# The order of all 3,359 operations of a clustered-attention and Mish-FFN kernel, taken from a written list

## The chip, the cores and the metric

The kernel runs on one core of a Trainium2 chip. The metric is the device time of one execution in microseconds, from the unprofiled runs; the profile is of one further execution.

## The reference, cut to what matters

Queries, keys and values have 4 batches, 8 heads, 768 positions and 64 features. Every query and key is assigned to one of 16 clusters of its head by the largest product of its normalised vector with the normalised centroids. A query attends to the keys of its own cluster. The result, 3072 tokens by 512, goes through a feed-forward block with a Mish-like gate of width 2048.

```python
    mask = q_assign[:, :, :, None] == k_assign[:, :, None, :]
    scores = scale * np.matmul(q, k.transpose(0, 1, 3, 2))
    scores = np.where(mask, scores, -1000000000.0)
    scores = scores - np.max(scores, axis=-1, keepdims=True)
    attn = np.exp(scores)
    attn = attn / (np.sum(attn, axis=-1, keepdims=True) + 1e-09)
    return np.matmul(attn, v).astype(np.float32)
...
    h = x @ w_in
    sp = np.where(h > 20.0, h, np.log1p(np.exp(np.minimum(h, 20.0))))
    g = h * np.tanh(sp)
    return (g @ w_out).astype(np.float32)
```

## The kernel before, in words

**Work.** A unit is one head of one batch and one of three blocks of 256 queries: 96 units, numbered 0 to 95, each with two halves of 128 queries. A product of two float32 matrices is made of float16 (or float32r) high and low parts, three matmuls for one. The operations of a half, `(i, a)`, in the order in which they need each other, with their first lines:

- `scores` (L625, PE): four matmuls into a two-bank PSUM tile, of which there are two. Its operands come from `prep_hi` (L477), `prep_lo` (L491) and copies by DMA or ACT (`copy_t`, `copy_z`, `copy_a`, `copy_b`, `hot_copy`); the cluster mask is an extra 16 rows made by the `assign_*` operations (L536 on).
- `rowmax` (L645, DVE), `expo` (L651, ACT, the Exp, with the row sum), `total` and `recip` (POOL or DVE, DVE).
- `p_hi` (L692, POOL) and `p_lo` (L704, DVE): high and low halves of the probabilities, and `ptrans` (L719), which transposes them by a DMA from the SP queue. For the first 24 units (pairs 0 to 11) `p_lo` transposes on PE instead, and `ptrans` copies from PSUM.
- `pv` (L737, PE): the product with the values, for a pair of units `m` (2m, 2m+1), in three parts of twelve matmuls; one PSUM tile.
- `pv_out` (L778, ACT) and `x_lo` (L806, DVE): the two halves of the feed-forward block's input.

The feed-forward block works on tiles of 256 tokens. `m1` (L818, PE) is half a tile of the hidden layer, twelve matmuls, two halves to a PSUM tile, of which there are two; `e_mish` (L836, ACT) applies Mish and frees the tile; `e_gh` (L847, POOL) and `e_gl` (L854, DVE) split it; `m2` (L957, PE) is one of eight parts of six matmuls that add up to an output tile; `m_out` and `m_store` write it. Hidden tiles `j` come in pairs: the even `e_mish` loads the Mish table first (L842), the odd one loads the Exp table behind it (L845). The last tiles, 72 to 95, use a Strassen-like scheme: sums of weight blocks (`c_whole`, `c_sums`, `c_high`, `c_low`, L1007 to L1037), sums of activations (`n_*`, `l_*`), and products `n_mul` (L906) and `k_mul` (L1106), whose results are combined and stored.

In the first 170 us the weights are also prepared: `w_load`, `w_abs`, `w_low`, `w_f32`, `w_sq` (a Gram matmul for the norm), `w_hi`, `w_lo`, and the centroids are normalised: `put_consts` (L154) makes constants, `centroids` (L178) and `cent_put` (L203) the operand for the assignment.

**Order.** Each operation is a small function, entered in a plan with a time key: a formula with constants of the tables `T` (L1371) and `N` (L1504), plus an entry of `SHIFT` (L1561), a dictionary with single corrections. The plan sorts by key and issues; a function that needs another's result calls `pl.after`, which issues that one first if it is still open. After every operation, `tie` pins each new instruction behind the last one of its engine (and DMA queue), so each of the five engines works in exactly the order of issue; what one engine waits for on another is left to semaphores.

```python
    def at(self, t, fn, *args):
        op = fn.__name__, *args
        self.ops[op] = (t + SHIFT.get(op, 0), len(self.ops), fn, args)
...
    def run(self):
        for op in sorted(self.ops, key=lambda op: self.ops[op][:2]):
            self.issue(op)
```

`ring` (L1001) is called by three functions of the tail that take a tile from the pool of three `pt` tiles; it issues the last user of the tile three before, if that is still open:

```python
    def ring(*last):

        while len(rings) >= 3 and pl.state.get(rings[-3]) != "done":
            pl.after(rings[-3])
        rings.append(last)
```

Of the kernel before, what the change touches and what calls it, by code (L numbers as in the profile page):

```python
# [25 lines left out]

class Plan:
# [27 lines left out]
    def tie(self):  # L55
# [17 lines left out]
def tile_clustered_attention_mish_ffn(  # L73
# [9 lines left out]
    nc = tc.nc  # L83
    pool = lambda name, bufs, **kw: ctx.enter_context(tc.tile_pool(name=name, bufs=bufs, **kw))
# [22 lines left out]
    pl = Plan(tc)  # L107
# [891 lines left out]
    rings = []  # L999

    def ring(*last):  # L1001

        while len(rings) >= 3 and pl.state.get(rings[-3]) != "done":
            pl.after(rings[-3])
        rings.append(last)

    def c_whole(f):  # L1007
        pl.after(("pv", NU // 2 - 1, 2), ("w_lo", 8 + f))
        ring("c_low", f)
# [96 lines left out]
    def k_mul(t, n, f):  # L1106
# [3 lines left out]
        if f == 0:  # L1110
# [3 lines left out]
            else:  # L1114
                banks(("k", t))
                ring("k_12", t)
# [1194 lines left out]
```

## Time and profile before

| | us |
|---|---|
| unprofiled runs: median of 3 (lowest to highest) | 856.79 (856.72 to 857.35) |
| span of the profiled execution | 858.6 |
| PE busy (matmuls) | 837.1 |
| DVE busy | 702.6 |
| ACT busy | 520.9 |
| POOL busy | 428.0 |

The profiled execution's own time is its span, first to last instruction; it stands 1.8 us above the median of the unprofiled runs. PE is TensorE's matmuls, DVE VectorE, ACT ScalarE, POOL GpSimd, SP the queue that issues most DMAs. An engine's idle time is shown with what ended it. The profile's busy time of PE counts a matmul to its modelled end, so two matmuls that overlap count once and a stall shorter than the tail of a matmul does not show.

### The profile page before, as it was taken

The page shows a single profiled execution, that of the slowest core. Times are in us where ns is not written, and L with a number is a line of the kernel's source. Part 1 is how long each engine was busy: PE and PEld are TensorE (multiplying, and loading weights), DVE is VectorE, ACT ScalarE, POOL GpSimd, SP SyncE. Part 2 cuts the span into 40 slices and gives each one's busy share as a digit, 9 for nine tenths or more (in the row PEclk, how much of TensorE's full clock was granted, in tenths as well). Part 3 has the DMA queues.
Part 4 walks back from the last instruction along what each step waited for, and adds up shares of the span by engine and source line. Part 5 has one row for each costly group of instructions (what it writes and reads, how often), then busy time and mean ns, then how long its engine had stood idle before and what let it go on. Part 6 is the DMA issues. An engine that isn't in the chain of part 4 may idle for free.

```text
span 858.6 us, 17602 instructions
## 1 busy us (share of the span) xinstructions
PE 837.1 (97%) x6742; PEld 621.0 (72%) x6743; DVE 702.6 (82%) x1225; ACT 520.9 (61%) x885; POOL 428.0 (50%) x410
## 2 busy tenths in 40 slices
PE   8999899999999999999999999999999999999998
PEld 3776676776777777776776776776777776788887
DVE  7989989898889798788877798788978777699851
ACT  6878887765665666564565665465565564356520
POOL 1464665786567546556566447566566444110000
PEclk9999999999999999999999999999999999999999
DMA  9855672398889987897789977988887876000010
GB/s 348 262 173 165 193 209 54 73 180 170 149 153 194 193 154 133 156 184 141 145 177 181 172 157 120 171 155 165 130 159 136 139 137 128 24 1 2 1 44 32
DMA packets 253060, 121.51 MB, mean 142 GB/s; under 512 B 230288, under 2 KB 230800, under 8 KB 252976
## 3 DMA queue, kind: packets, MB, share of 16 engines
q1 hardware_dynamic: 247632, 108.46, 61.1%
q10 hardware_dynamic: 5344, 11.93, 6.3%
q8 instruction: 53, 0.87, 0.4%
q14 instruction: 31, 0.25, 0.1%
HBM read 35.72 MB, written 6.29 MB: 49 GB/s over the span
## 4 chain that ended last, share of the span: by engine, by line
PE 70%; DVE 13%; issue 5%; ACT 4%; DMA 4%; POOL 3%; ACTq 0%; POOLq 0%; DVEq 0%; SPq 0%
PE h L832 8%; PE h L833 8%; PE h L834 8%; PE o L753 8%; PE O L969 6%; PE O L971 6%; PE O L970 6%; PE s L631 5%; PE s L636 5%; DVE m L648 4%; PE cn L922 2%; DVE hl L717 2%; DMA pt<-hl 2%; ACT p L662 2%; PE as L543 1%
## 5 line engine op out<-in xcount | busy, mean ns | idle before, releaser
L662 ACT ACTIVATE p<-s,m 128x768 f32<-128x768 f32 x192 | 172.6, 899 | 161.4 <-DVE m L648 108.0
L700 POOL TENSOR_SCALAR hl<-p,l 128x768 f16<-128x768 f32 x144 | 167.1, 1163 | 168.0 <-DVE l L682 74.2
L648 DVE TENSOR_REDUCE m<-s 128x1 f32<-128x768 f32 x192 | 181.4, 949 | 30.2 <-PE s L636 28.1
L717 DVE SCALAR_TENSOR_TENSOR hl<-p,l,hl 128x768 f16<-128x768 f32 x144 | 172.4, 1202 | 12.2 <-POOL hl L700 11.7
L832 PE MATMUL h<-x,w 128*128 128x256 f16 x640 | 175.6, 274 | 1.5 <-ACT u L843 0.8
L833 PE MATMUL h<-x,w 128*128 128x256 f16 x640 | 174.4, 273 | 0.0
L834 PE MATMUL h<-x,w 128*128 128x256 f16 x640 | 174.4, 273 | 0.0
L631 PE MATMUL s<-A,B 128*128 128x384 f32 x384 | 117.3, 386 | 1.8 <-DMA B<-T 0.8
L969 PE MATMUL O<-w,g 128*128 128x512 f16 x288 | 109.6, 380 | 0.0
L971 PE MATMUL O<-w,g 128*128 128x512 f16 x288 | 109.2, 379 | 0.0
L970 PE MATMUL O<-w,g 128*128 128x512 f16 x288 | 109.2, 379 | 0.0
L636 PE MATMUL s<-Z,T 80*128 80x384 f32 x384 | 99.2, 339 | 0.4 <-issue 0.4
L832 PEld LDWEIGHTS <-w 128*128 128x128 f16 x768 | 75.1, 98 | 26.9 <-issue 17.3
L849 POOL TENSOR_SCALAR g<-u,mscg 128x512 f16<-128x512 f32 x72 | 70.3, 980 | 38.4 <-ACT u L843 36.0
L857 DVE SCALAR_TENSOR_TENSOR g<-u,mscg,g 128x512 f16<-128x512 f32 x72 | 75.5, 1050 | 12.2 <-POOL g L849 11.9
L833 PEld LDWEIGHTS <-w 128*128 128x128 f16 x768 | 75.5, 98 | 11.1 <-issue 1.6
L753 PE MATMUL o<-pt,v 128*64 128x256 f16 x1296 | 79.3, 274 | 3.6 <-DMA pt<-hl 3.0
L834 PEld LDWEIGHTS <-w 128*128 128x128 f16 x768 | 75.2, 98 | 8.6
L753 PEld LDWEIGHTS <-v 128*64 128x64 f16 x1296 | 68.4, 110 | 14.1 <-issue 9.6
L631 PEld LDWEIGHTS s<-A,B 128*128 128x128 f32 x384 | 61.9, 190 | 15.8 <-issue 4.9
L636 PEld LDWEIGHTS s<-Z,T 80*128 80x128 f32 x384 | 69.7, 189 | 0.9 <-DMA Z<-stg 0.7
L843 ACT ACTIVATE u<-h,msch 128x512 f32<-128x512 f32 x80 | 52.1, 685 | 25.0 <-PE h L834 14.5
(242 smaller groups left out, 1366.3 us busy)
## 6 DMA issues: line engine op xcount, KB each, us to landing
qk<-in_qk_dram SPq DMA_DIRECT2D x32, 384.0 KB, 4.6
stage<-in_w_in_dram SPq DMA_DIRECT2D x16, 512.0 KB, 6.6
stage<-in_w_out_dram SPq DMA_DIRECT2D x16, 512.0 KB, 4.5
vraw<-in_vP_dram SPq DMA_DIRECT2D x16, 384.0 KB, 5.2
T<-A ACTq DMA_DIRECT2D x30, 192.0 KB, 3.0
Z<-B SPq DMA_DIRECT2D x30, 192.0 KB, 3.4
B<-T ACTq DMA_DIRECT2D x28, 192.0 KB, 3.4
out_dram<-osb SPq DMA_DIRECT2D x18, 256.0 KB, 2.7
```

The lines of the kernel that those rows point to most:

```text
L631: nc.tensor.matmul(s[:, j, :384], st["B", n][:, q0 : q0 + P], st["A", n][:, j * 384 : (j + 1) * 384], start=True, stop=False,)
L636: nc.tensor.matmul(s[:, j, :384], st["T", n][: D + NCL, q0 : q0 + P], st["Z", n][: D + NCL, j * 384 : (j + 1) * 384], start=False, stop=True,)
L648: nc.vector.tensor_reduce(m, st["s", i, a][:, :, :384], axis=AX.XY, op=ALU.max, negate=True)
L662: nc.scalar.activation(p.rearrange("p (n x) -> p n x", n=2), st["s", i, a][:, :, :384], AF.Exp, bias=st["m", i, a], scale=1.0, accum_out=l,)
L700: nc.gpsimd.tensor_scalar(t[:, 0], p, r, 1.0, op0=ALU.mult, op1=ALU.mult)
L717: nc.vector.scalar_tensor_tensor(t[:, 1], p, r, t[:, 0], op0=ALU.mult, op1=ALU.subtract)
L753: nc.tensor.matmul(o[s * D : s * D + D, :256], v if early else v[:, int(part == 1)], st["pt", 2 * m + s][:, :, c + (0 if early or part < 2 ...
L832: nc.tensor.matmul(o, wh, xh, start=(c == 0), stop=False)
L833: nc.tensor.matmul(o, wh, xl, start=False, stop=False)
L834: nc.tensor.matmul(o, wl, xh, start=False, stop=(c == 3))
L969: nc.tensor.matmul(o, gh, wh, start=(f == 0 and fi == 0), stop=False)
L970: nc.tensor.matmul(o, gh, wl, start=False, stop=False)
```

## The change

The time keys and `SHIFT` (728 lines) are replaced by one list, `ORDER`, with all 3,359 operations; an operation's key is its place in the list. `ring` and its three calls go. Pools are wrapped in a class `Ring`, which notes each request for a tile, so that `tie` can pin the first instruction behind a request after the first instruction behind the one before from the same pool and tag, also where the two are on different engines. Work, shapes, engines and tiles of every operation stay. The formulas for the keys stay in the text but are no longer used.

```diff
+class Ring:
...
+    def tile(self, *args, tag=None, **kw):
+        if tag is None:
+            return self.pool.tile(*args, **kw)
+        self.asked.append((len(self.traced), (id(self), tag)))
+        return self.pool.tile(*args, tag=tag, **kw)
...
-        self.ops[op] = (t + SHIFT.get(op, 0), len(self.ops), fn, args)
+        self.ops[op] = (RANK[op], len(self.ops), fn, args)
...
-        for ins in self.traced[self.seen :]:
+        for n, ins in enumerate(self.traced[self.seen :], self.seen):
+            while self.asked and self.asked[0][0] <= n:
+                _, key = self.asked.pop(0)
+                if self.taken.get(key, ins.name) != ins.name:
+                    self.tc.add_manual_dep(ins, self.taken[key], order, reason="tile order")
+                self.taken[key] = ins.name
...
-        ring("c_low", f)
...
-        ring("l_sl", f)
...
-                ring("k_12", t)
...
-SHIFT = {
-    ('expo', 11, 0): -0.001, ('w_load', 10): -0.351, ('pv_out', 18): -0.443, ('scores', 24, 1): -0.221,
...
+ORDER = """
+qk_load 1, qk_load 0, qk_load 3, qk_load 2, centroids, put_consts, cent_put, prep_hi 1, prep_lo 1, prep_hi 0, v_load 0
+1, v_load 0 3, w_load 1, w_load 3, w_load 0, v_load 0 2, assign_mm 0, prep_lo 0, copy_z 1, copy_z 0, assign_turn 0,
+assign_max 0, assign_hot 0, assign_back 0, assign_put 0, copy_t 0, copy_a 0, copy_t 1, v_sq 0 3, copy_a 1, hot_direct
+1, copy_b 0, w_abs 1, v_sq 0 1, hot_direct 0, w_abs 3, v_sq 0 2, w_abs 0, w_load 2, v_load 0 0, w_load 7, w_load 4,
...
+w_f32 10, w_f32 13, w_f32 9, recip 5 1, w_f32 17, rowmax 7 1, w_abs 14, ptrans 6 0, rowmax 7 0, qk_load 6, copy_z 3,
...
+0, x_lo 21, p_hi 23 0, p_lo 23 0, scores 24 0, v_scale 1, rowmax 24 0, recip 23 1, ptrans 23 0, copy_t 9, moe_scale_h
+0, expo 24 0, m1 0 0, total 20 0, recip 20 0, prep_lo 9, p_hi 23 1, v_high 0 0, v_split 0 0, p_lo 23 1, v_split 0 1,
+rowmax 24 1, total 24 0, recip 24 0, ptrans 23 1, w_hi 14, expo 24 1, w_lo 14, pv 11 0, pv 11 1, total 21 0, recip 21
...
+recip 26 0, total 26 1, e_gl 0, rowmax 27 0, e_gl 1, recip 26 1, m2 0 0 0, scores 28 0, m1 3 1, m2 0 0 1, scores 27 1,
+total 23 0, recip 23 0, expo 27 0, copy_t 10, e_mish 2, e_mish 3, p_hi 26 0, prep_lo 10, p_hi 26 1, total 27 0, rowmax
+28 0, p_lo 26 0, v_split 1 0, recip 27 0, rowmax 27 1, ptrans 24 1, qk_load 13, ptrans 25 1, ptrans 25 0, copy_z 10,
+p_hi 27 0, v_high 1 1, e_gh 2, e_gh 3, pv 12 0, pv 12 1, pv 12 2, m1 4 0, m1 5 0, m1 4 1, expo 28 0, copy_b 10, pv_out
...
+recip 19 0, e_mish 4, expo 28 1, copy_a 10, expo 29 0, total 28 1, p_lo 28 0, recip 28 1, total 29 0, rowmax 29 1,
+recip 29 0, m1 7 0, scores 30 1, m1 5 1, scores 31 0, pv 13 0, pv 13 1, pv 13 2, m1 7 1, scores 30 0, m1 6 0, m1 6 1,
+scores 31 1, expo 29 1, e_mish 5, e_gh 4, p_hi 28 1, prep_hi 11, p_hi 29 0, p_lo 28 1, total 29 1, rowmax 30 1, rowmax
...
+RANK = {}
+for _n, _op in enumerate(" ".join(ORDER.split()).split(", ")):
+    _name, *_args = _op.split()
+    RANK[_name, *map(int, _args)] = _n
```

## Rows read from the trace of the kernel before

**Rows 1.** The page, first part: span, then each engine's busy time.

```profile
span 858.6 us, 17602 instructions
...
PE 837.1 (97%) x6742; PEld 621.0 (72%) x6743; DVE 702.6 (82%) x1225; ACT 520.9 (61%) x885; POOL 428.0 (50%) x410
```

**Rows 2.** Stretches: length, busy time by engine, granted clock, DMA share, GB/s.

```profile
0.00:27.80 27.80, 23.46 (x129) 12.79 (x130) 22.80 (x52) 20.32 (x38) 5.76 (x15) 1.00 0.93 336
27.80:157.80 130.00, 122.39 (x964) 89.55 (x963) 119.34 (x222) 105.04 (x209) 74.37 (x90) 1.00 0.55 161
157.80:177.60 19.80, 18.59 (x148) 14.67 (x147) 18.70 (x28) 13.75 (x23) 14.70 (x14) 1.00 0.68 114
...
200.00:740.00 540.00, 536.21 (x4288) 386.36 (x4287) 437.28 (x729) 317.25 (x517) 310.01 (x272) 1.00 0.83 153
740.00:820.00 80.00, 80.00 (x718) 69.99 (x716) 74.23 (x146) 45.23 (x71) 4.35 (x6) 1.00 0.01 5
```

**Rows 3.** Waits of PE, 200 to 740 us: total, times, longest.

```profile
PE o L753 <- DMA pt<-hl: 2.6, 3, 1.3
PE s L631 <- DMA B<-T: 0.8, 1, 0.8
```

**Rows 4.** Waits of DVE, 20 to 160 us: total, times, longest.

```profile
DVE m L648 <- PE s L636: 3.3, 4, 1.0
DVE l L680 <- POOL l L674: 1.9, 2, 1.0
```

**Rows 5.** Timeline of DVE, 0 to 24 us: start, duration, operation, idle before.

```profile
4.47 0.22 DVE L181 TENSOR_TENSOR csq<-csb 128x64 f32<-128x64 f32 x1 [0.83 <-DMA csb<-in_cent_dram]
...
9.92 0.98 DVE L554 STREAM_TRANSPOSE D<-as 128x768 f32<-128x768 f32 x1 [0.18 <-PE as L543]
```

**Rows 6.** Timeline of ACT, 4 to 20 us.

```profile
5.51 0.92 ACT L481 ACTIVATE A<-qk,scq 128x768 fp32r<-128x768 f32 x1
...
7.65 0.26 ACT L207 COPY C<-ct 64x128 f32<-64x128 f32 x1 [0.36 <-PE ct L201]
```

**Rows 7.** Timeline of DVE, 45 to 54 us.

```profile
48.26 0.17 DVE L680 RECIPROCAL l<-l 128x2 f32<-128x2 f32 x1 [0.90 <-POOL l L674]
...
51.51 0.96 DVE L648 TENSOR_REDUCE m<-s 128x1 f32<-128x768 f32 x1 [0.89 <-PE s L636]
```

**Rows 8.** Timeline of PE, 496 to 503 us: a pv, then two m2.

```profile
497.85 2.15 PE L753 MATMUL o<-pt,v 128*64 128x256 f16 x36
499.94 0.39 PE L969 MATMUL O<-w,g 128*128 128x512 f16 x1
...
502.54 0.27 PE L832 MATMUL h<-xx,w 128*128 128x256 f16 x1
```

**Rows 9.** Timeline, 454 to 463.5 us: an m1 half, a scores, the next m1.

```profile
455.54 0.28 PE L832 MATMUL h<-x,w 128*128 128x256 f16 x1
...
456.78 0.59 PE L631 MATMUL s<-A,B 128*128 128x384 f32 x2
...
457.57 0.28 PE L832 MATMUL h<-x,w 128*128 128x256 f16 x1
```

**Rows 10.** The page, fifth part: groups, count | busy, mean ns | idle before.

```profile
L662 ACT ACTIVATE p<-s,m 128x768 f32<-128x768 f32 x192 | 172.6, 899 | 161.4 <-DVE m L648 108.0
L700 POOL TENSOR_SCALAR hl<-p,l 128x768 f16<-128x768 f32 x144 | 167.1, 1163 | 168.0 <-DVE l L682 74.2
...
L849 POOL TENSOR_SCALAR g<-u,mscg 128x512 f16<-128x512 f32 x72 | 70.3, 980 | 38.4 <-ACT u L843 36.0
```

**Rows 11.** The chain that ended last, in order of time: start, duration, what.

```profile
456.86 5.70 DMA pt<-hl
```

**Rows 12.** Timeline of ACT, 476 to 483 us: an Exp, then a pair of e_mish.

```profile
479.29 0.19 ACT L662 ACTIVATION_READ_ACCUMULATOR p<-s,m 128x1 f32 x1
479.49 1.28 ACT L842 ACT_TABLE_LOAD   x1
480.79 1.26 ACT L843 ACTIVATE u<-h,msch 128x512 f32<-128x512 f32 x2
```

More of the change, by code (lines that the diff above doesn't have):

```diff
@@ new lines @@
+copy_t 7, w_abs 31, total 13 0, recip 13 0, rowmax 18 1, recip 16 1, rowmax 18 0, recip 17 1, w_f32 31, ptrans 17 1,
+w_sq 30, pv 8 0, w_sq 31, w_sum 1, expo 18 0, p_hi 18 0, p_lo 18 0, scores 19 0, w_spread 1, expo 18 1, ptrans 18 0,
+v_sq 1 0, v_sq 1 3, p_hi 18 1, w_scale 1, rowmax 19 0, p_lo 18 1, scores 19 1, pv 8 1, pv 8 2, total 18 1, w_hi 8,
+rowmax 19 1, ptrans 18 1, recip 18 1, expo 19 0, expo 19 1, pv_out 16, pv_out 17, w_lo 8, total 19 1, qk_load 8,
+v_load 1 2, copy_z 7, hot_copy 7, qk_load 9, qk_load 10, assign_mm 2, p_hi 19 0, assign_turn 2, prep_hi 8, prep_lo 8,
@@ new lines @@
+18 0, m1 18 1, scores 43 1, m1 20 0, m2 1 1 5, pv_out 38, pv_out 39, expo 42 0, expo 42 1, v_sq 2 1, copy_t 15, x_lo
+38, x_lo 39, total 42 0, p_lo 40 0, rowmax 43 0, total 42 1, p_lo 41 1, v_split 1 3, e_gl 16, recip 42 0, recip 42 1,
+scores 44 1, m2 1 1 6, assign_mm 4, p_hi 42 1, p_hi 42 0, p_lo 42 1, rowmax 43 1, ptrans 41 1, ptrans 40 0, ptrans 42
+1, v_load 2 0, hot_copy 15, expo 43 0, e_mish 18, copy_a 15, expo 43 1, e_gl 17, total 43 0, recip 43 0, p_lo 42 0,
+total 43 1, recip 43 1, assign_turn 4, rowmax 44 1, pv 20 0, p_hi 43 1, e_gh 18, p_hi 43 0, prep_hi 16, prep_lo 16, pv
@@ new lines @@
+52 0, m_out 2 1, expo 52 1, scores 53 0, m1 28 1, m2 3 0 0, scores 53 1, m1 29 0, m1 29 1, p_lo 51 1, e_gl 26, total
+52 0, p_lo 50 1, total 52 1, recip 52 1, e_gl 27, rowmax 53 1, recip 52 0, rowmax 53 0, ptrans 51 0, ptrans 50 0,
+copy_z 18, ptrans 51 1, hot_copy 18, ptrans 50 1, copy_b 18, expo 53 1, e_mish 28, e_mish 29, expo 53 0, m2 3 0 1, pv
+25 0, pv 25 1, pv 25 2, p_hi 52 1, p_hi 52 0, prep_hi 19, prep_lo 19, e_gh 29, pv_out 50, scores 54 0, m2 3 0 2,
+scores 54 1, m1 30 0, m1 31 0, m2 3 0 3, scores 55 0, m1 30 1, scores 55 1, m1 31 1, p_lo 52 0, p_lo 52 1, total 53 0,
@@ new lines @@
+32 0, pv 32 1, pv 32 2, m2 4 1 5, scores 68 1, m1 43 0, m1 43 1, m2 4 1 6, scores 68 0, m2 4 1 7, m1 45 0, m1 44 0, m1
+44 1, pv_out 64, pv_out 65, copy_b 23, e_mish 42, e_mish 43, p_hi 67 0, p_hi 67 1, e_gh 43, prep_hi 24, e_gh 42, e_gl
+40, p_lo 67 0, x_lo 65, v_split 2 3, assign_turn 6, assign_max 6, p_lo 67 1, x_lo 64, rowmax 68 1, assign_hot 6,
+rowmax 68 0, assign_back 6, expo 68 1, m_out 4 1, expo 68 0, copy_t 24, assign_put 6, scores 69 0, m2 5 0 0, total 68
+0, total 68 1, recip 68 1, recip 68 0, e_gl 42, assign_stg 6, prep_lo 24, p_hi 68 0, p_hi 68 1, scores 69 1, m1 45 1,
@@ new lines @@
+recip 79 0, p_hi 79 0, e_gh 54, e_gh 55, ptrans 76 0, qk_load 29, ptrans 77 0, copy_z 27, ptrans 77 1, hot_copy 27,
+ptrans 76 1, ptrans 78 0, m2 6 0 5, scores 80 0, pv 38 0, pv 38 1, pv 38 2, copy_b 27, p_lo 79 0, e_gl 54, rowmax 80
+0, total 79 1, p_lo 78 1, e_gl 55, recip 79 1, assign_mm 7, m2 6 0 6, scores 80 1, copy_a 27, expo 80 0, pv_out 76,
+pv_out 77, p_hi 79 1, prep_hi 28, prep_lo 28, x_lo 76, x_lo 77, total 80 0, assign_turn 7, p_lo 79 1, rowmax 80 1, m1
+59 0, scores 81 1, m2 6 0 7, scores 81 0, m1 56 0, m1 56 1, m2 6 1 0, scores 82 0, m2 6 1 1, m_store 5 1, ptrans 79 0,
@@ new lines @@
+copy_t 30, e_mish 62, e_mish 63, pv_out 84, pv_out 85, expo 87 1, expo 88 0, e_gh 63, prep_lo 30, p_hi 87 0, e_gh 62,
+x_lo 85, x_lo 84, e_gl 62, p_lo 87 0, total 87 1, total 88 0, recip 87 1, e_gl 63, rowmax 88 1, recip 88 0, p_hi 88 0,
+p_hi 87 1, rowmax 89 0, p_lo 88 0, p_lo 87 1, ptrans 86 0, ptrans 86 1, copy_z 30, hot_copy 30, ptrans 87 0, copy_a
+30, ptrans 87 1, expo 88 1, e_mish 64, copy_b 30, m2 7 0 6, scores 89 1, m2 7 0 7, m1 65 0, total 88 1, recip 88 1,
+rowmax 89 1, m_out 7 0, expo 89 0, expo 89 1, p_hi 88 1, prep_hi 31, m1 65 1, m2 7 1 0, scores 90 0, m2 7 1 1, scores
```

973 lines of the change are left out of this document (282 added, 691 removed), and 37 rows, old and new, of the table SHIFT.

## The prediction

> **What bounds the kernel now.** I read the page's first part first, for the engine that is never free: PE is busy for 837.1 of 858.6 us, so at most 21.5 us of idle time is there to be won by any order [rows 1]. Busy is not the same as streaming (a matmul's end is modelled), so the second view was the table of stretches, to see where PE stands still. It splits the run in three. Up to 177.6 us PE stands for 4.3, 7.6 and 1.2 us, 13.2 in all, while DVE works 22.8 of 27.8, 119.3 of 130 and 18.7 of 19.8: there PE and DVE bound together, and an idle microsecond of DVE is a late microsecond of PE. From 200 to 740 us PE stands for only 3.8 of 540 us and DVE has 103 us to spare; from 740 to 820 PE never stands, and DVE is busy for 74.2 of 80 [rows 2]. The granted clock is at its upper level (1.00, 2.4 GHz) throughout, so the clock has nothing to give [rows 2]. Third, the waits: of PE's in the long middle stretch 2.6 us is for transposed probabilities that have not landed and 0.8 us for a copied operand [rows 3]; of DVE's early ones the longest are for scores from PE (3.3 us, four times) and for row sums from POOL (1.9 us, twice) [rows 4].
>
> So an order can win three things: DVE's waits before 160 us, the hand-over to the steady part at 157 to 178 us, and the 3.4 us of DMA waits behind it. The count of work is unchanged: the same 3,359 operations, the same matmuls, transfers and tiles.
>
> **The change, part by part.** In the new list every operation stands behind all that it needs, so nothing is pulled forward when it is issued: the engines get the list as written. I compared it with the order that the old keys give, engine by engine. It is a near relative: before every pv of the first twelve pairs the list asks DVE for the same work within 1.5 us.
>
> *Head, loss.* `put_consts` now stands behind `centroids` on DVE, and `centroids` begins only when its load lands, at 4.47 us [rows 5]; the constants' 1.1 us, done before that now, come after. On ACT both `prep_hi` stand behind `cent_put`: the first of them ran at 5.51 us, in the hole before `cent_put` at 7.65 us [rows 6], and the new list leaves that hole empty. DVE then takes both `prep_lo` (1.0 us each) and both `copy_z` (0.56) before `assign_turn 0`, which so starts near 11.9 instead of 9.92 us [rows 5]. But `prep_lo 1` and `copy_z 1` are thereby out of the way of later DVE work. Counted in DVE idle time the head loses some 0.7 us, counted at the first row maximum 1.5; I take +1.0, ends 0 and 2.
>
> *DVE waits, 28 to 158 us, gain.* Two waits of 0.90 and 0.89 us stood in front of `recip 5 1` and `rowmax 7 1` [rows 7]. The new list puts three `w_f32` in front of the first and one behind it, work that has to be done anyway, so both should go. The 1.0 us in front of `rowmax 24 1` gets a `recip`, a 0.56 us copy and a scale ahead of it. Three smaller ones get fillers too; those in front of `rowmax 19 1`, `recip 18 1` and `assign_turn 2` keep their order and should stay. That is 3.8 us removed if nothing else opens; another order opens waits that the old trace cannot show. I take half, -1.9, ends -3.8 and +2.
>
> *Hand-over, gain.* Before `pv 12 0` the new list has one `m2` piece (1.30 us) and one `scores` (0.79) more on PE [rows 8, 9], 2.1 us of work in front of the place where PE waited, and DVE has the same work. POOL has four operations fewer there: two `e_gh` at 0.98, one `p_hi` at 1.16 [rows 10] and one `prep_hi`, about 5 us; the `p_hi` that are left feed the `p_lo` and transposes of pv 12. I take -2.0, the PE work, ends -4 and 0.
>
> *Transfers in the steady part, gain.* A pv needs the transposes of four row blocks, 5.7 us from issue to use where PE waited for them [rows 11]. What hides this chain is the PE work listed between the last `scores` of a pair and its pv. For pv 30 the old order has five m1 halves, two m2 pieces, four scores and a pv: 5 x 1.24 + 2 x 1.30 + 4 x 0.79 + 2.15 = 14.1 us [rows 8, 9]; the new one six, four, six and one, 19.5 us. Over the 36 pairs the mean goes from 17.5 to 19.2 us, and those under 15 us from nine to three. Against that stand three pairs that lose 2.5 to 4.3 us from long distances. The bound is the 3.4 us of rows 3; I take half, -1.7, ends -3.4 and +3.4.
>
> *Activation tables, loss.* The old order keeps the two `e_mish` of a pair together, with one load of the Mish table before and one of the Exp table behind. The new list puts an Exp (`expo`) between them in 17 places (`e_mish 4, expo 28 1, ... e_mish 5` is the first), so 34 loads are added. One is 1.28 us, and the instructions on both sides follow within 0.03 us [rows 12]: 34 x 1.28 = 43.6 us of ACT, covered only by its idle time. ACT stands for 0.84 us on average in front of an `expo` (161.4 us over 192) [rows 10], so a load exposes some 0.44 us, 7.5 us over 17 exps, and these meet chains that have just become 1.7 us longer in PE work. I take +1.0; ends 0 and 7.5, and 21.8 if all 17 reach PE whole.
>
> The Trainium skill (ScalarE: Activation LUTs, section What ACT_TABLE_LOAD costs) states a drain of about 1.38 us besides the 1.28 us of a load. By it the 34 switches would take about 90 us of ACT, an estimate from that page. The trace shows no drain around its loads, so it does not bear that out, and the sum goes by the row.
>
> *PSUM buffers of m1, loss.* There are two, and the old order never has less than 2.6 us of PE work between a finished tile and the next m1 but once; the new has ten places with a single m1 half, 1.24 us [rows 9]. The reader, a Mish of 0.63 us [rows 12], fits; behind a table load of 1.28 it misses by 0.7, and three places outside the tail are such. +0.5, ends 0 and 5.
>
> *Tail, loss.* `n_mul 0 1` waits for `c_low 0`, which in the new list has 29 us of DVE work between it and the last `x_lo`; PE has 36 us listed between the last pv and that n_mul. With ACT's part in between (a Mish, a high half) the slack is about 1 us, where DVE is busy 93% of the time [rows 2]. +0.5, ends 0 and 4. The last eight k_mul, the last store and what follows them are as before: nothing.
>
> Removing `ring` and adding `Ring` only orders instructions when the program is built; no instruction comes of it: nothing.
>
> **Sum:** 1.0 - 1.9 - 2.0 - 1.7 + 1.0 + 0.5 + 0.5 = -2.6 us on the profiled 858.6, so 856.0; the median of the unprofiled runs is 856.79, 1.8 below that span, which makes 854.2.
>
> **Rivals.** *Nothing gained* (within 0.2%, 1.7 us, about what a measurement of this kernel can tell from no change): DVE's early waits move instead of going, and the longer chains only pay for the tables. For it speaks that DVE is at 92% there and that its work before each pv is unchanged; against it that two fillers are plain to see. 856.8.
>
> *Slower, by the tables.* Place: the 17 pairs between 170 and 725 us. Price: without the table term the sum is -3.6; it turns to slower by over 0.2% once more than 5.3 us of the 43.6 reaches PE, that is 0.3 us a pair. At 7.5 us the time is 860.7, and it would be 865 or more if PE's single-half m1 buffers wait behind the same loads. For it: ACT works strictly in its list, and 68 exps (40 before) stand behind an operation that needs later PE work. Against it: ACT was busy for 317 of 540 us [rows 2].
>
> *Much faster.* All fillers hold and all steady waits go, no loss shows: -3.8 - 4.0 - 3.4 = -11.2, 845.6. Against it the head, which is plain.
>
> **How the numbers follow.** Forecast 0.42 and much faster 0.10 make faster 0.52; nothing gained 0.24; slower 0.24, of which tables 0.18 and tail or buffers 0.06. The range 847 to 863 reaches most of the way to both outer cases and takes in the ends of the small terms; about 0.1 is left out on either side.
>
> **What would show it.** Head: `assign_turn 0` near 11.9 us and the first Exp near 20.3. Early part: DVE's wait for POOL's row sums near 1.0 us instead of 1.9, pv 12 about 2 us earlier. Middle: 34 more table loads, ACT busy near 564 us, PE's wait for transposes under 1.5 us. Tail: PE without a gap over 1 us after 740 us. The forecast is wrong if PE's waits on ACT (m1 behind Mish, scores behind Exp) add up to more than 5 us between 170 and 725 us, or if PE stands as long before 178 us as now.

## The result, and the profile after

The changed kernel takes 864.51 us (863.91 to 865.24, 4 runs), the kernel before on the same chip 857.07 us (856.72 to 858.13): ratio 1.0078, interval 1.0055 to 1.0101, **6.7 us slower** (the two medians lie 7.4 us apart; the ratio is the measure used below). The forecast was 854.2 with a range up to 863.

The profiled execution's span is 862.2 us and its own time 863.91, so this kernel's time is its span plus 1.7. The span of before, 858.6 us, would by that be an execution of 860.3, 3.5 us above the median of 856.8 that the forecast started from; that execution's own time is not on record. The forecast took the span to be 1.8 above the kernel's time. A second profile of the old order (the run old_list below) has a span of 855.9 and a time of 857.6; the comparisons here go against that one.

In the code of the changed kernel nearly all lines named in the prediction stand 24 further down: L655/L660 are `scores`, L686 the `expo`, L734 the transposes of `p_lo`, L753/L755 the copies of `ptrans` (DVE and ACT), L777 `pv`, L867 Mish. First the page's first part: span, then each engine's busy time and instructions.

```profile
span 862.2 us, 17574 instructions
PE 834.7 (97%) x6743; PEld 623.9 (72%) x6743; DVE 689.2 (80%) x1225; ACT 566.1 (66%) x919; POOL 409.2 (47%) x410
```

ACT has 34 instructions and 45.2 us more; PE is busy for 2.4 us less in a span 3.6 longer [rows 1]. The same stretches as in [rows 2]:

```profile
0.00:27.80 27.80, 22.37 (x115) 11.99 (x116) 21.02 (x49) 20.06 (x36) 5.32 (x14) 1.00 0.85 309
27.80:157.80 130.00, 121.13 (x973) 90.84 (x970) 123.67 (x221) 103.50 (x206) 74.23 (x90) 1.00 0.57 168
157.80:177.60 19.80, 17.93 (x137) 13.55 (x138) 17.56 (x31) 14.24 (x24) 14.08 (x14) 1.00 0.58 93
177.60:200.00 22.40, 19.86 (x162) 15.38 (x162) 20.69 (x34) 17.75 (x25) 15.76 (x14) 1.00 0.96 180
200.00:740.00 540.00, 534.33 (x4313) 389.10 (x4308) 425.94 (x738) 361.87 (x554) 292.30 (x273) 1.00 0.80 154
740.00:820.00 80.00, 80.00 (x700) 68.26 (x698) 67.05 (x133) 43.31 (x67) 6.06 (x7) 1.00 0.00 1
```

From 27.8 to 157.8 us DVE's idle time fell from 10.7 to 6.3 us, and yet PE's rose from 7.6 to 8.9. From 200 to 740 us PE stands for 5.7 us instead of 3.8. The waits tell by whom. Waits of DVE, 20 to 160 us (total, times, longest), those that answer to [rows 4]:

```profile
DVE l L704 <- POOL l L698: 0.3, 1, 0.3
DVE m L672 <- PE s L660: 0.2, 1, 0.2
```

A longer one is new, for ACT's part of `pv_out`:

```profile
DVE xf L822 <- ACT rb L821: 2.0, 4, 0.9
```

Waits of PE, 20 to 160 us, first the longest ones before, with the two for copies of `ptrans`, then those of the changed kernel for these copies:

```profile
PE q L710 <- ACT p L662: 2.9, 8, 0.9
PE gram L296 <- DVE w L276: 2.4, 3, 1.4
PE q L710 <- DVE pt L729: 1.0, 3, 0.5
PE q L710 <- ACT pt L731: 0.7, 2, 0.6
```

```profile
PE q L734 <- ACT pt L755: 4.4, 5, 1.8
PE q L734 <- DVE pt L753: 3.8, 5, 2.4
```

Waits of PE, 200 to 740 us, which answer to [rows 3]:

```profile
PE s L655 <- ACT p L686: 3.4, 5, 0.8
PE o L777 <- DMA pt<-hl: 1.7, 2, 1.0
PE as L567 <- ACT p L686: 1.0, 1, 1.0
```

DVE's two early waits went from 5.2 to 0.5 us, and PE no longer waits for `w_f32` in front of a Gram matmul (2.4 us before), but PE's waits for the copies of `ptrans` went from 1.7 to 8.2 us. In the steady part PE waits 4.4 us behind an exp, a wait of 0.2 us in the old order.

**How late PE is.** To compare kernels whose operations stand in another order I took, for each PE operation, its start less the usual times of all PE operations listed ahead of it (the 30th percentile of the time to the next start, by kind of operation and neighbours, over the profiles of both kernels). The result is PE's lateness in us. Each value is the mean over 10 us; the two runs on the right are explained below.

| at | old order | changed | no added loads | loads written out early |
|---|---|---|---|---|
| 28 us | 17.5 | 17.6 | 17.7 | 18.6 |
| 100 | 30.4 | 32.5 | 32.6 | 34.9 |
| 160 | 37.4 | 38.5 | 38.9 | 40.4 |
| 200 | 41.0 | 43.2 | 42.4 | 44.1 |
| 350 | 42.4 | 48.8 | 45.8 | 48.2 |
| 500 | 43.6 | 51.4 | 46.6 | 49.7 |
| 740 | 46.4 | 53.8 | 49.8 | 50.4 |
| 820 | 49.1 | 55.5 | 51.8 | 52.4 |

The changed kernel is 1.1 us later than the old order at 160 us, 2.2 at 200, 6.4 at 350 and at 820. At the end this agrees with the spans, 862.2 - 855.9 = 6.3. Most of the loss arises between 200 and some 350 us, where four waits for an exp end (at 223, 308, 324 and 354 us). The first and the third stand in the kernel without added loads too (at 222 and 321 us, 0.53 and 0.80 us), so they are not the loads' doing.

### The profile page after: what moved, and what is told of

Same layout as the page of the kernel before. It is cut to its first block, busy times and chain, and to the rows that moved or that the text cites. A ratio compares the mean times of both kernels' runs of the same rounds, so it can differ in the third digit from the quotient of the medians.

```text
span 862.2 us, 17574 instructions
## 1 busy us (share of the span) xinstructions
PE 834.7 (97%) x6743; PEld 623.9 (72%) x6743; DVE 689.2 (80%) x1225; ACT 566.1 (66%) x919; POOL 409.2 (47%) x410
## 5 line engine op out<-in xcount | busy, mean ns | idle before, releaser
L686 ACT ACTIVATE p<-s,m 128x768 f32<-128x768 f32 x192 | 172.8, 901 | 110.7 <-DVE m L672 55.3
L724 POOL TENSOR_SCALAR hl<-p,l 128x768 f16<-128x768 f32 x144 | 156.0, 1086 | 188.1 <-DVE l L706 87.7
L741 DVE SCALAR_TENSOR_TENSOR hl<-p,l,hl 128x768 f16<-128x768 f32 x144 | 174.5, 1218 | 24.5 <-POOL hl L724 23.9
L857 PE MATMUL h<-x,w 128*128 128x256 f16 x640 | 174.4, 273 | 0.0
L655 PE MATMUL s<-A,B 128*128 128x384 f32 x384 | 124.4, 405 | 5.8 <-ACT p L686 4.6
L660 PE MATMUL s<-Z,T 80*128 80x384 f32 x384 | 99.2, 339 | 0.2 <-DVE T L627 0.2
L655 PEld LDWEIGHTS s<-A,B 128*128 128x128 f32 x384 | 65.1, 190 | 29.7 <-ACT p L686 11.9
L857 PEld LDWEIGHTS <-w 128*128 128x128 f16 x768 | 75.3, 98 | 9.9
L777 PE MATMUL o<-pt,v 128*64 128x256 f16 x1296 | 78.2, 274 | 3.3 <-DMA pt<-hl 3.3
L873 POOL TENSOR_SCALAR g<-u,mscg 128x512 f16<-128x512 f32 x72 | 60.9, 850 | 39.2 <-ACT u L867 33.5
L777 PEld LDWEIGHTS <-v 128*64 128x64 f16 x1296 | 68.1, 110 | 13.8 <-issue 10.7
L867 ACT ACTIVATE u<-h,msch 128x512 f32<-128x512 f32 x80 | 53.9, 687 | 28.2 <-PE h L858 22.5
L660 PEld LDWEIGHTS s<-Z,T 80*128 80x128 f32 x384 | 69.9, 189 | 0.5 <-ACT w L283 0.5
L881 DVE SCALAR_TENSOR_TENSOR g<-u,mscg,g 128x512 f16<-128x512 f32 x72 | 60.2, 843 | 5.1 <-POOL g L873 5.0
```

Of the source, the lines that this page charges most:

```text
L655: nc.tensor.matmul(s[:, j, :384], st["B", n][:, q0 : q0 + P], st["A", n][:, j * 384 : (j + 1) * 384], start=True, stop=False,)
L660: nc.tensor.matmul(s[:, j, :384], st["T", n][: D + NCL, q0 : q0 + P], st["Z", n][: D + NCL, j * 384 : (j + 1) * 384], start=False, stop=True,)
L686: nc.scalar.activation(p.rearrange("p (n x) -> p n x", n=2), st["s", i, a][:, :, :384], AF.Exp, bias=st["m", i, a], scale=1.0, accum_out=l,)
L724: nc.gpsimd.tensor_scalar(t[:, 0], p, r, 1.0, op0=ALU.mult, op1=ALU.mult)
L741: nc.vector.scalar_tensor_tensor(t[:, 1], p, r, t[:, 0], op0=ALU.mult, op1=ALU.subtract)
L777: nc.tensor.matmul(o[s * D : s * D + D, :256], v if early else v[:, int(part == 1)], st["pt", 2 * m + s][:, :, c + (0 if early or part < 2 ...
```

## The experiments

Ratios are to the kernel before; 0.001 is 0.86 us. A difference of two ratios is uncertain by some 1.3 to 2.5 us, by their intervals. TensorE's granted clock is 1.00 (2.4 GHz) up to 820 us in the profiles of old_list, of the changed kernel and of new_no_loads; where a stretch of another profile shows less, part of it ran at the lower level (1.2 GHz); where that bears on a reading it is said below.

### The list form, and what 34 loads cost in the old order

```diff
 ORDER = """   # old_list: the order that the kernel before issues
...
+        if j in SPLIT:   # old_loads: 17 odd j
+            nc.scalar.preload_act_table_set("natural_log_exp_and_others")
+            nc.scalar.preload_act_table_set("mish")
         nc.scalar.activation(st["u", j], st["h", j], AF.Mish, ...)
```

> The list form of the changed kernel, filled with the order that the kernel before issues (all 3,359 operations, written out). Both theories: the same work in the same order, so the ratio to the kernel before is 1.000, within 0.002; if the list form itself costs something, 1.005 or more. It also gives a second profile of the old order. The first had a span of 858.6 us; the changed kernel's own time is 1.7 us above its span, and if that holds here too this one's span should be near 855.3, and some of the waits shown before (1.49 us at pv 30, 1.19 at assign_mm 5, 1.40 at pv 12) should be shorter or gone.

> The old order, with 34 table loads more: in the same 17 pairs an Exp load and a Mish load are put in front of the odd e_mish. Nothing else is moved. Theory of the tables (the loads are what made the change slower): 44 us of ACT of which 4 to 7 us reach PE, 861 to 864 us, ratio 1.005 to 1.008. Rival (ACT has the time, the order of the other work is what costs): under 1.5 us, ratio 1.000 to 1.002.

> The old order with 17 loads more instead of 34: only one (Mish) in front of the odd e_mish of the same 17 pairs. The pair of loads there, 2.57 us, cost 34 us in all, 2.0 us a place. Theory of the slack (each place hides the same 0.55 us, the rest is paid in full): 1.28 - 0.55 = 0.73 us a place, 12.4 us, 869 to 871, ratio 1.0145. Rival (a load costs 1.0 us wherever it stands in the old order): 17 us, ratio 1.020. Rival (there is a threshold above one load): under 5 us, ratio under 1.006.

old_list: 1.0007 (0.9997 to 1.0018), so the list form costs nothing that can be measured. Its waits of PE, 200 to 740 us:

```profile
PE o L777 <- DMA pt<-hl: 1.1, 2, 0.6
PE as L567 <- DMA qk<-in_qk_dram: 0.6, 1, 0.6
PE s L655 <- ACT p L686: 0.2, 1, 0.2
```

The waits for transfers are 1.7 us here, 3.4 in the first profile [rows 3], with the same order. Half of what I wanted to win in the steady part belonged to that one execution.

old_loads: 891.69 us, 1.0401 (1.0386 to 1.0416), **34 us**. Both the theory and its rival were far too low. With half of the loads: 869.21 us, 1.0137 (1.0116 to 1.0159), 11.7 us, where the theory of the slack said 12.4. So at one of the 17 places the first load of 1.28 us costs 0.69 and the second (34.4 - 11.7) / 17 = 1.34: some 0.6 us of the first are hidden, and of the second nothing. Waits of PE in old_loads, 200 to 740 us:

```profile
PE s L655 <- ACT p L686: 13.8, 12, 2.3
PE o L777 <- DMA pt<-hl: 2.8, 5, 1.1
```

PE stands behind exps. ACT is busy for 64% of that stretch; that says nothing about these places. The same stretch in the view of rows 2:

```profile
200.00:740.00 540.00, 519.09 (x4068) 368.91 (x4066) 417.82 (x696) 346.48 (x529) 298.37 (x265) 0.99 0.79 148
```

PE stands for 20.9 of 540 us, 1.9 in old_list. The granted clock counts too: behind a wait of 2.33 us for an exp, at 497.5 us, part of PE's work ran at the lower level, and in all the clock was 0.94 from 480 to 540 us and 0.96 from 620 to 660. By estimate (0.06 x 60 + 0.04 x 40) that is up to 5 of the 34 us, and it would explain that the second load costs more than its 1.28 us; with half of the loads the clock stays at 1.00. It is not shown how much of it reached the end.

### The new list without its added loads

```diff
-            ... AF.Exp,
+            ... AF.Identity if (i, a) in PLAIN else AF.Exp,   # new_no_loads: 34 halves, new_four_places: 11
```

> The new list unchanged in its order. The 34 exps that stand between the two e_mish of a pair apply Identity in place of Exp, a function that both tables hold, so the 34 added table loads go and nothing else (what is left out: these 34 halves are not exponentiated). Theory of the tables in its new, smaller form (the waits of PE behind a late exp at 305, 321, 351, 451 and 673 us of the changed kernel, 5.4 us in all, come from the loads): 4 to 5.5 us of 7 come back, 859 to 860.5, ratio 1.002 to 1.004. Theory of the loads at their full price in the old order (1.0 us each, 34 us): it would gain over 20 us. Rival (order alone): under 1.5 us, ratio 1.006 or more.

> The new list with Identity for Exp in 11 exps only, those between the e_mish of four pairs (4 and 5, 18 and 19, 24 and 25, 36 and 37; these halves are not exponentiated): 8 of the 34 added loads go, 26 stay. Theory (the loads cost where the profile shows PE waiting behind a late exp or its transposes, at 198, 305, 351 and 451 us of the changed kernel, 4.2 us by the difference of PE's lateness): 3.5 to 4.5 us come back, ratio 1.0025 to 1.004. Rival (the cost is spread evenly, 0.17 us a load): 1.3 us, ratio 1.005 to 1.0065.

new_no_loads: 859.01 us, 1.0012 (1.0002 to 1.0022). 33 of the 34 loads are gone, and 1.0078 - 1.0012 = 0.0066, **5.7 of the 6.7 us** (3.5 to 7.8), with them. By the two profiles it is 4.0 us of span (862.2 and 858.2): PE stands for 1.5 us less from 177.6 to 200 us and for 2.5 less from 200 to 740. Exps that apply Identity take as long as before (900 ns). Its waits of PE, 200 to 740 us:

```profile
PE s L655 <- ACT p L686: 2.2, 4, 0.8
PE as L567 <- ACT p L686: 0.6, 1, 0.6
PE s L655 <- DMA A<-A: 0.4, 1, 0.4
```

Here no `pv` waits for its transposes any more, as forecast, but 2.8 us of waits for exps stand where the old order has 0.2. Freed of its loads the new steady part is no faster than the old one.

new_four_places: 860.87 us, 1.0036 (1.0022 to 1.0050), 3.6 us back. A quarter of the loads (8 of 34) holds some 63% of their cost, where an even spread would give 1.3 us, the lower end of what the two intervals leave: it sits where PE stands. Of PE's waits from 200 to 740 us, those at 308, 354 and 454 us (1.04, 0.79 and 0.78 us) are gone in this profile.

### Moving the pairs together

```diff
-..., e_mish 16, total 40 0, ..., expo 41 1, e_mish 17, ...
+..., e_mish 16, e_mish 17, total 40 0, ..., expo 41 1, ...
```

> The new list, with the two e_mish of a pair put side by side again in 13 of the 17 places (the odd one moved up behind its m1, or the even one moved down, and the exps between them put ahead or behind): 26 of the 34 added table loads go, all else stays in its order. Theory of the tables: 3 to 5 of the 7 us come back, 859.5 to 861.5, ratio 1.003 to 1.005. Rival (order of the other work): no gain beyond 1 us, ratio 1.007 to 1.009.

new_pairs: 898.60 us, 1.0473 (1.0446 to 1.0500). ACT has 26 loads fewer and the kernel is 34 us slower than with them. Waits of PE, 200 to 740 us:

```profile
PE s L655 <- ACT p L686: 15.4, 8, 3.1
PE h L856 <- ACT u L867: 7.3, 2, 4.4
```

To put two Mish side by side, exps or a Mish had to leave their place. ACT works in its list, so whatever is put ahead holds up all behind it while it waits for its own input: PE now waits up to 4.4 us for a Mish to free an m1 buffer. The granted clock is 0.98 from 200 to 740 us here (0.91 from 320 to 380, behind a wait of 3.14 us for an exp), so a part of the 34 us is PE's work at the lower level. The experiment answers the question that it was made for only in part (it also moves work), but it shows that the loads were not to be saved this way. The Trainium skill (ScalarE: Activation LUTs, section Table sets: the hidden batching unit) has the rule to batch activations by set. The old order keeps to it pair by pair and is the faster one; made afterwards in the new list by these moves, the batching costs more (34 us) than the 26 loads that it saves.

### Where a load stands

What the loads wait for is in the view of groups. ACT in the changed kernel, count | busy, mean ns of one | idle time before, releasers:

```profile
L866 ACT ACT_TABLE_LOAD x37 | 47.5, 1283 | 2.3 <-POOL A L511 1.6
L869 ACT ACT_TABLE_LOAD x36 | 46.2, 1283 | 0.6
L686 ACT ACT_TABLE_LOAD x17 | 21.8, 1283 | 9.7 <-DVE m L672 7.2 <-DVE hl L741 1.3 <-DVE l L698 1.0
L867 ACT ACT_TABLE_LOAD x17 | 21.8, 1283 | 2.0 <-DVE g L881 1.1 <-DVE l L698 0.6
```

The 73 loads written in the code (L866, L869) stand behind 2.9 us of idle time, the 17 that the build put in front of an exp (L686) behind 9.7, of which a row maximum ended 7.2. **The load waits for the input of its exp.** One place, ACT's timeline, 303 to 308 us:

```profile
303.37 0.69 ACT L867 ACTIVATE u<-h,msch 128x512 f32<-128x512 f32 x1
304.08 0.83 ACT L536 CAST A<-A 64x768 fp32r<-64x768 f32 x1
305.84 1.28 ACT L686 ACT_TABLE_LOAD   x1 [0.92 <-DVE m L672]
307.13 0.90 ACT L686 ACTIVATE p<-s,m 128x768 f32<-128x768 f32 x1
```

PE's timeline, the row that waits for this exp:

```profile
308.18 1.50 PE L567 MATMUL as<-qk,C 128*32 128x512 f32 x16 [1.04 <-ACT p L686]
```

ACT stands for 0.92 us, and then, when the row maximum is there, loads for 1.28. So these loads cannot use ACT's idle time, which is what my estimate let them do.

```diff
+        if j in TO_MISH:
+            nc.scalar.preload_act_table_set("mish")
         nc.scalar.activation(st["u", j], st["h", j], AF.Mish, ...)
+        if j in TO_EXP:
+            nc.scalar.preload_act_table_set("natural_log_exp_and_others")
```

> The new list, all computed, with the 34 added loads written out: an Exp load directly behind the first Mish of each of the 17 pairs and a Mish load directly ahead of the second. The number of loads is the same (108); they no longer stand behind the wait of the exp. Theory (the loads cost because they begin only when the exp's row maximum is there; 9.7 us of idle time lies ahead of the 17 Exp loads, 0.9 to 1.0 us at the places where PE waited): 2.5 to 4 us of the 5.7 come back, ratio 1.003 to 1.005. Rival (ACT's sum of work is what counts, 566 us either way): no gain, 1.006 or more.

> The new list with Identity for Exp between the e_mish of a pair (those halves are not exponentiated), and in the same 17 pairs 34 loads put back in the form in which they cost 34 us in the old order: an Exp and a Mish load in front of the odd e_mish. Theory that the new list has more slack on ACT at these places: 5 to 8 us on top of the 859 without them, 864 to 867, ratio 1.007 to 1.010. Rival (what makes the loads of the changed kernel cheap is that they stand apart, one ahead of an exp and one ahead of the Mish): 880 or more, ratio 1.025 and over.

new_early_loads: 860.72 us, 1.0020 (1.0003 to 1.0036). With the same 108 loads **5.0 of the 5.7 us** (2.5 to 7.4) are back, more than the 2.5 to 4 that I expected; what is left, 0.7 us, can't be told from nothing. The same place, ACT's timeline:

```profile
303.90 0.69 ACT L869 ACTIVATE u<-h,msch 128x512 f32<-128x512 f32 x1
304.61 1.28 ACT L871 ACT_TABLE_LOAD   x1
305.90 0.83 ACT L536 CAST A<-A 64x768 fp32r<-64x768 f32 x1
306.76 0.90 ACT L686 ACTIVATE p<-s,m 128x768 f32<-128x768 f32 x1
```

and PE's:

```profile
307.80 1.50 PE L567 MATMUL as<-qk,C 128*32 128x512 f32 x16 [0.15 <-ACT p L686]
```

The load fills the hole, and PE's wait falls from 1.04 to 0.15 us. That this profile is late from the start (the table above) is for the most part the clock: 0.94 in the first 27.8 us and 0.99 from there to 157.8, by estimate (0.06 x 27.8 + 0.01 x 130) up to 3.0 us. From 200 to 820 us its PE loses 8.3 us, as in the old order (8.1); without the loads it loses 9.4, in the changed kernel 12.3.

new_lumps, both loads in front of the odd Mish (the form of old_loads) in the new list: 873.05 us, 1.0155 (1.0130 to 1.0180), 12 us above the list without loads. Its six times lie in two groups, 868 to 869 and 873 to 874 us, so the 12 is rough. Neither theory had it (5 to 8, or over 20). The same 34 loads thus cost 34 us in the old order and 12 in the new one in the same form, 5.7 where the build put them, and 0.7, not to be told from nothing, ahead of the waits.

### The two halves of the run

```diff
-ORDER: new
+ORDER: old up to an operation, then all others as in the new list (new_then_old: the reverse)
```

> The new list up to pv 11 (159 us), then all that is left in the old order: no table load is added. Theory of the tables: the loss of the head (0.6 us) and little else, ratio 1.000 to 1.002. Rival (the loss is made in the first 160 us, where the new order's waits of PE for transposed probabilities came to 8 us against 2): 1.003 to 1.008.

> The old order up to pv 11 (157 us), then what is left in the new order, with its 34 added loads. Theory: the new first part cost 1 us by the profile at 160 us, so the time is 863 to 864, ratio 1.006 to 1.007. Rival (it cost the whole 3.4 us that the new first part followed by the old order showed): 860 to 861.5, ratio 1.003 to 1.004.

> As the one before, with Identity for Exp in the exps that stand between the e_mish of a pair (those halves are not exponentiated). If the parts add, the new steady part alone, freed of its loads: the gain of the kernel with the new list throughout (4 to 5.5 us) on top of old_then_new, 857.5 to 860, ratio 1.000 to 1.003. If the steady part holds the gain that was forecast for it once the loads are gone (1.7 us of transfers), 0.998 to 1.000.

> The old order up to pv 0 (27.5 us), then the new list. The forecast took the new head at a loss of 1.0 us: ratio 1.0065 to 1.007. Rival (the head's delay is made up by DVE before the steady part, or the new order behind it does not fit the old head): no change or worse, 1.008 and over.

| | us | ratio (interval) |
|---|---|---|
| new to pv 11, then old | 861.54 | 1.0040 (1.0025 to 1.0056) |
| old to pv 11, then new | 863.57 | 1.0065 (1.0051 to 1.0079) |
| the same, without added loads | 858.18 | 1.0005 (0.9994 to 1.0016) |
| old to pv 0, then new | 863.49 | 1.0075 (1.0057 to 1.0094) |

From the changed kernel the old first part takes 1.1 us off with the loads (0.0013) and 0.6 without (0.0007). Neither is clear of noise, but the lateness at 160 us says the same, 1.1. The head alone can't be told apart from nothing. new_then_old is 3.4 us slower, as its rival had it, although PE is only 0.9 us later at 200 us: the rest, 2.5 us, comes along the steady part, where that profile has more waits for transposes (3.0 us). With the 5.6 us of the reverse the halves make 9.0, more than the 6.7 of the whole. So they do not add, and why is open.

### The copies behind DVE's fillers

DVE's timeline in the changed kernel, 85 to 90 us:

```profile
85.49 1.71 DVE L371 SCALAR_TENSOR_TENSOR w<-w,ws0r,w 128x1024 f16<-128x1024 f32 x1
87.12 2.29 DVE L300 SCALAR_TENSOR_TENSOR w<-w,stage 128x512 uint32<-128x512 uint32 x1
89.34 0.55 DVE L753 COPY pt<-q 128x384 f32<-128x384 f32 x1
```

PE's timeline, its next transposes:

```profile
89.94 0.55 PE L734 MATMUL q<-ident,p 128*128 128x128 f32 x3 [2.36 <-DVE pt L753]
```

The copy frees a PSUM buffer for PE. The new list puts a `w_lo` (L371) and a `w_f32` (L300) ahead of it, and PE stands for 2.36 us.

```diff
-..., w_f32 21, expo 11 1, copy_t 5, ptrans 11 0, ...
+..., ptrans 11 0, w_f32 21, expo 11 1, copy_t 5, ...
```

> The new list, with the copies of the transposed probabilities out of PSUM (ptrans) of units 7 to 12 moved up directly behind their p_lo, as the old order has them; in the new list up to 29 operations stand between, w_f32, w_lo, pv_out and row maxima on DVE. Theory (the fillers that took DVE's waits away hold up these copies, and PE waits for the buffer: 8.2 us of such waits up to 160 us against 1.7): PE's waits for the copies fall by 4 us or more, the lateness of PE at 100 us by about 2 us, the end by 1 to 2 us: ratio 1.0055 to 1.0065. Rival (DVE is the bound there and its row maxima only come later): no gain, 1.007 to 1.009, DVE's waits for scores back near 3 us.

> The new list with two copies (ptrans) of unit 8, half 0, and unit 11, half 0, moved ahead of the DVE work that the new list put in front of them: the first ahead of a row maximum, the norm of a weight block and a w_f32 (4 us of DVE), the second ahead of one w_f32 (2.3 us). Their transposes are on PE by then, so DVE does not have to wait. Theory (the fillers hold up the copies, and PE waits for the buffer: 1.86 us at 67.9 and 2.58 us at 86.8): these two waits go, PE's lateness at 100 us falls by 1.5 to 3 us, and the end by up to 1 us: ratio 1.0065 to 1.0075. Rival (DVE's own work is the bound; the waits come back behind other work): no change at 160 us.

new_ptrans, which moves all copies of six units: 873.71 us, 1.0177 (1.0159 to 1.0196), worse by 8.5 us. Its waits of DVE, 20 to 160 us, first line:

```profile
DVE pt L753 <- PE q L734: 9.7, 8, 4.1
```

Directly behind `p_lo` in the list, these copies now come before PE has done the transposes, and DVE waits in front of them, 9.7 us instead of 0.9. The stretch in the view of rows 2:

```profile
27.80:157.80 130.00, 116.33 (x897) 88.22 (x897) 113.80 (x199) 96.95 (x193) 66.73 (x83) 0.95 0.57 164
```

PE stands for 13.7 us instead of 8.9, and the granted clock is 0.95 instead of 1.00. It is 0.54 from 74 to 81.5 and from 91 to 98.5 us, each time behind a stretch in which PE stood: it was busy for 11.4 of the 14.0 us and for 5.5 of the 9.5 us before. By estimate (0.05 x 130) up to 6.5 us are PE's work at the lower level. So this run says nothing for or against the fillers. new_fillers moves only two copies, whose transposes were done: 862.70 us, 1.0039 (1.0025 to 1.0053), 3.3 us better. PE's waits for copies, 20 to 160 us:

```profile
PE q L734 <- ACT pt L755: 2.7, 5, 0.9
PE q L734 <- DVE pt L753: 2.2, 5, 0.7
```

They fell from 8.2 to 4.9 us. At 160 us, though, PE is hardly earlier than in the changed kernel (38.4 against 38.5), at 820 us by 1.1. The granted clock hides a part in this profile, 0.91 from 60 to 80 us where the changed kernel has 1.00, by estimate up to 1.8 us (0.09 x 20). The gain is real by the interval; that all of it comes through these two waits is not shown.

### All together

> The old order up to pv 11, then the new list, with the 34 loads written out as in the kernel with early loads; all is computed. If the parts add: 1.0065 less the same gain, 1.002 to 1.004. Rival (no gain from the place of the loads): 1.0065.

> Both changes together, all computed: the 34 loads written out ahead of the waits, and the two copies (ptrans 8 0 and 11 0) ahead of DVE's fillers. Theory (two separate causes, so the gains add): 1.0020 less 1.3 to 3.3 us, ratio 0.998 to 1.0005. Rival (they overlap): 1.002.

> As the one before, and expo 45 0 one place up on ACT, ahead of v_sq 2 3 (0.84 us), which stands between e_mish 19 and that exp and for which PE's scores 46 1 wait at 321 us. Theory: 0.8 to 1.1 us less at that place, ratio 0.997 to 0.9995. Rival: the exp waits for its row maximum instead, no gain.

> The old order up to pv 11, the new list behind it with the loads written out (1.0010 so far), and the same exp ahead of v_sq 2 3. Theory: 0.8 to 1.1 us less, ratio 0.9995 to 1.0005. Rival: no gain, 1.001.

```diff
-..., v_sq 2 3, expo 45 0, ...
+..., expo 45 0, v_sq 2 3, ...
```

| | us | ratio (interval) |
|---|---|---|
| old to pv 11, then new, loads early | 858.96 | 1.0010 (0.9996 to 1.0023) |
| new, loads early, two copies ahead | 859.24 | 1.0010 (0.9997 to 1.0024) |
| the same, expo 45 0 ahead of v_sq 2 3 | 860.50 | 1.0024 (1.0008 to 1.0040) |
| old to pv 11, then new, loads early, the same exp ahead | 860.08 | 1.0021 (1.0007 to 1.0034) |

With both causes taken out the new list can't be told from the kernel before. I expected 1.0005 or less from both together; by the interval of 1.0010 it is open whether the two gains add. The exp that I moved ahead of a square gained nothing: it now waits 1.29 us for its row maximum, and PE waits 0.80 us at that place as before. No version here beats the kernel before.

## Why the prediction was wrong

**Activation tables: the step that failed.** Count (34) and busy time (45.2 us more, 43.6 forecast) were right, and the rival "slower, by the tables" named the mechanism with its point of decision: over 5.3 us of them reach PE. 5.7 did by the ratios (3.5 to 7.8), 4.0 by the two profiles. I took +1.0 with 7.5 as the upper end, and no row stands behind that choice. What I got wrong is the cover: I set 1.28 us of load against 0.84 us of idle time ahead of an average exp [rows 10], as if the load could run in it. The loads that the build inserts run after that idle time; written out early, they cost 0.7 us (0.0008), not to be told from nothing or from my +1.0. As to the drain that the Trainium skill (ScalarE: Activation LUTs, section What ACT_TABLE_LOAD costs) states besides the load, the trace still shows none: the load at 305.84 ends at 307.12, and its exp starts at 307.13.

The loads are half of the miss. Without them the list stands 1.0 us above the kernel before (1.0012), where my sum without the table term was -3.6: 4.7 us of the miss are the loads and 4.6 are gains that did not come, as follows. Of my two signs that the forecast is wrong the second showed: PE stands for 16.2 us before 177.6 us instead of 13.2. The first did not quite: PE's waits on ACT between 170 and 725 us are 4.4 us, not over 5.

**DVE waits, -1.9: right about DVE, wrong about PE.** The fillers did what was forecast: the two kinds of wait fell from 5.2 to 0.5 us, and DVE's idle time, with 2.0 us of new waits, by 4.4. But the sentence at the start, that an idle microsecond of DVE is a late microsecond of PE, does not hold there. The fillers stand ahead of copies that free PE's buffers; PE's waits for them rose from 1.7 to 8.2 us, more than the waits for `w_f32` (2.4 us) and for exps (2.9 to 1.0) gave, and at 160 us PE is 1.1 us later instead of 0.9 earlier (the head's +1.0 with -1.9). I read the old order's DVE waits as the price for short ways to PE; new_fillers bears that out for two copies. I named who waits for DVE's row maxima, not who waits for its copies.

**Head, +1.0: inside its ends.** `assign_turn 0` starts at 12.11 us (11.9 forecast), the first Exp at 20.51 (20.3).

**Hand-over, -2.0: did not come.** The PE work in front of pv 12 is there, but the last `p_lo` for it ends later by about as much: 1.9 us. The last row of `p_lo` ahead of pv 12 on DVE's timeline, first in the old order, then in the changed kernel:

```profile
171.85 1.65 DVE L741 SCALAR_TENSOR_TENSOR hl<-p,l,hl 128x768 f16<-128x768 f32 x1
```

```profile
174.03 1.40 DVE L741 SCALAR_TENSOR_TENSOR hl<-p,l,hl 128x768 f16<-128x768 f32 x1
```

It ends at 173.50 and 175.43. From 160 to 200 us PE loses 3.6 us in the old order, 4.7 in the new, 3.5 in the new without loads: no gain, and 1.2 us for the first pair that a load splits. POOL's lighter list was no help, since DVE's place for `p_lo` set the end.

**Transfers in the steady part, -1.7: gained, and given back.** Without added loads PE's waits for transfers there are 0.4 us, against 1.7 (old_list) and 3.4 [rows 3]. The longer distances work. The 2.8 us of waits for exps take it back.

**PSUM buffers of m1, +0.5, and tail, +0.5: not seen.** From 200 to 740 us no m1 waits for a Mish, and from 740 to 820 PE has no gap; its lateness grows by 1.7 us there against 2.7 in the old order, a gain of 1.0.

**The base.** The profiled execution of before was a late one, if its time is its span plus 1.7, as in the other profiles, and not the span. Taking 1.8 off led to the right median, but the rows from which I took the gains then held 3.5 us that the median does not have.

## What to carry to other kernels

Idle time in front of an instruction covers extra work only if that work is issued ahead of the wait; the 17 table loads that the build put in front of an exp here stood behind it, so write the load out where the engine is idle. Before an idle gap of one engine is filled, look which of its instructions behind the filler free a buffer for the engine that bounds the kernel. And in an order without slack the busy share of an engine prices nothing: 34 loads of 1.28 us cost 0.7 us (not to be told from nothing), 5.7, 12 or 34 by their place and the order around them. A long wait of PE can cost twice: behind those of 2.33 us in old_loads and 3.14 us in new_pairs the granted clock fell to its lower level, behind the 2.36 us at 90 us in the changed kernel it did not.

## What the runs showed that I had not expected

The waits for transfers in the steady part, 3.4 and 1.7 us, differ by a factor of two between two profiles of one order; for a term of 2 us one profile is not enough.

The same instructions got shorter in the new order: the high half of g on POOL (L849 before, L873 after) 980 to 850 ns, its low half on DVE (L857, L881) 1050 to 843, `p_hi` on POOL 1163 to 1086 [rows 10]. In all DVE is busy for 13.4 us less and POOL for 18.8. The groups after:

```profile
L724 POOL TENSOR_SCALAR hl<-p,l 128x768 f16<-128x768 f32 x144 | 156.0, 1086 | 188.1 <-DVE l L706 87.7
L873 POOL TENSOR_SCALAR g<-u,mscg 128x512 f16<-128x512 f32 x72 | 60.9, 850 | 39.2 <-ACT u L867 33.5
L881 DVE SCALAR_TENSOR_TENSOR g<-u,mscg,g 128x512 f16<-128x512 f32 x72 | 60.2, 843 | 5.1 <-POOL g L873 5.0
```

The traces show that these slow down where both engines work at once. The low half on DVE takes 738 ns before and 741 after where POOL does hardly anything meanwhile (16 and 33 of the 72), 1341 and 1121 where POOL works all the time (30 and 9). The high half on POOL takes 691 and 694 ns with DVE idle (7 and 6), 1050 and 904 with DVE busy throughout (33 and 34). So the low half gained by overlapping less. What the two engines compete for is not shown. The shorter times brought nothing: neither engine is what PE waits for in the steady part.
